# Local attention heads in blocks of 32 queries by 64 keys, two heads transposed together, with the maxima subtracted on VectorE

## The chip, the cores and the metric

The kernel runs on one core of one Trainium2 chip. Five engines work side by side, each through its own list of instructions in order: TensorE (PE in the profile, its weight loads PEld), VectorE (DVE), ScalarE (ACT), GpSimd (POOL) and SyncE (SP), which issues most of the transfers. The metric is the device time of one execution in microseconds (us), lower is better: the median of several runs.

## What is computed

Sparse attention over 8 batches of 576 tokens with 8 heads of 64 elements, then a mixture of 8 experts with the two best per token. Half of the heads are *local*: a query sees itself and the 31 keys before it. The other half are *strided*: a query sees the earlier keys with the same position modulo 32.

```python
# q, k, v: (8, 8, 576, 64) float32; stride = 32; scale = 1 / sqrt(64)
scores = scale * np.matmul(q, k.transpose(0, 1, 3, 2))
rel = pos[:, None] - pos[None, :]
mask_local = (rel >= 0) & (rel < stride)
mask_strided = (rel >= 0) & (pos[None, :] % stride == pos[:, None] % stride)
masks = [mask_local if h < H // 2 else mask_strided for h in range(H)]
scores = np.where(masks, scores, -1e9)
scores = scores - np.max(scores, axis=-1, keepdims=True)
attn = np.exp(scores)
attn = attn / (np.sum(attn, axis=-1, keepdims=True) + 1e-09)
attn_out = np.matmul(attn, v)

# x: attn_out as (4608, 512); noisy top-2 of 8 experts
noisy = x @ w_gate + np.log1p(np.exp(x @ w_noise)) * noise
# out = sum over the two best experts e: weight * (relu(x @ w1[e]) @ w2[e])
```

## The kernel before

**One planned program.** Every step of the kernel is a `Piece` with an engine (or "ANY", which is ACT or DVE), an assumed duration, the tiles that it reads and writes, and a rank. `issue_all` is a list scheduler that runs while the program is built: it takes the piece that can start first by the assumed durations and writes its instructions at the end of that engine's list. So each engine has a fixed order that follows from the planned durations, and on the chip it goes through it in order. A change of one assumed duration can change the order of much else. The eight banks of PSUM are given out piece by piece. When the plan has TensorE wait in the first 170 us, it puts in matmuls of zeros (L401).

**Attention.** A unit is two heads of one batch, local or strided; there are 32 units, four to a batch (two local, two strided), and 16 of them are local. For a unit, `loads` (L435) fetches q, k and v; `prep` (L491) transposes q and k on TensorE so that the head dimension lies on partitions, with the first head on partitions 0 to 63 and the second on 64 to 127. After a batch's four units `route` computes the gate (L785), the two best experts and the place of each token in the experts' lists, and scatters 12 groups of entries from POOL (L875).

For a local unit the program does this:

- The values of the two heads are loaded in one transfer (L493) to partitions 32 to 95, in 18 blocks of 64 tokens (9 for each head); one copy (`front`, L317 on ACT or L320 on DVE, 32 partitions by 17 x 64 elements) puts the last 32 tokens of each block in front of the next, on partitions 0 to 31. A block of 64 queries so has 96 keys.
- `products` (L587 to 618) writes the mask into two banks of PSUM, one for each head, with bfloat16 matmuls (L601: 6 of them, of 96, 384 and 480 columns), and adds the scores (L608: 18 matmuls of 64 queries by 96 keys). These are matmuls on a quarter of the array, 64 rows by 64 columns; the two heads use the two halves of its rows, even and odd blocks the two halves of its columns. TensorE runs a float32 matmul as two instructions, so the trace has 36.
- `item` (L620 to 702) runs for each head. DVE takes the maxima of five groups of 96 scores (L635). ACT makes the exponentials with the maximum as bias, which is one number for each partition, so every group has an instruction of its own (L639, four for each head; L641, two more of 64 partitions, which put the last group of both heads into the second head's tile). TensorE transposes the groups (L649, four for the first head, five for the second), ACT or DVE copies the result out of PSUM (`aT`, L317 or L320), TensorE multiplies by the values and a column of ones (L668, 8 matmuls for each head with 96 rows by 64 columns of the array; L673, 2 more for the last group), and DVE adds 1e-9 to the sums (L678, L680), takes reciprocals (L683, L685) and scales (L689, L697) into `xo`.
- `finish` stores `xo` (L714) and transposes it for the gate (L735, L739).

The strided units go through the same `item`, with 72 keys instead of 96.

**Experts.** Seven jobs of the experts need only the tokens of earlier batches. Their matmuls (first layer L1317, second L1397) are filled in between those of attention from the fourth batch's gate on, and after the last gate the rest follows. Later jobs use a first layer with fewer products (L1221).

## Time and profile before

| | |
|---|---|
| median of 3 runs | 1063.34 us (1061.49 to 1064.67) |
| the profiled execution | 1060.7 us, of which the span of the program is 1058.7 us |
| mean granted TensorE clock | 0.991 of full speed |
| TensorE, VectorE, ScalarE, GpSimd busy | 98%, 69%, 50%, 51% of the span |
| moved by the transfers | 134.43 MB, 127 GB/s over the span |
| gates of the eight batches begin at | 43.1, 73.6, 103.5, 135.1, 175.5, 215.5, 258.2, 302.6 us |
| first matmul of an expert | 136.5 us |

Busy time of an engine is the share of time in which it has an instruction under way. Matmuls are pipelined and their ends in the trace are modelled, so the time that TensorE spends on something is read from the starts: from the first start of a group of matmuls to the start of whatever comes next. In rows of the timeline the columns are the start, the time from first start to last end, the engine, the line, the operation, out<-in, the form and the number of instructions merged in the row. In rows that group instructions the last numbers are the busy time in us, the mean duration of one in ns, and the idle time before them.

### The profile page before, as it was taken

What the parts mean: (1) busy time and instruction counts of PE and PEld (TensorE: products, weight loads), DVE (VectorE), ACT (ScalarE), POOL (GpSimd) and SP (SyncE); (2) the same over time, 40 slices, a digit from 0 to 9 for tenths busy, and PEclk for the clock granted to TensorE, in tenths of its full rate; (3) what the DMA queues carried; (4) which work ended last, traced back from release to release, by engine and by line L of the source; (5) the groups of instructions that cost most, each with busy time, mean ns of one, the idle gap of its engine ahead of it and who ended that gap; (6) DMA issues with size and microseconds to landing.
All of it is one profiled execution on the core that took longest, in us unless ns stands there. A gap on an engine that the chain in (4) does not pass through costs nothing.

```text
span 1058.7 us, 23340 instructions
## 1 busy us (share of the span) xinstructions
PE 1032.9 (98%) x8465; PEld 907.9 (86%) x8465; DVE 726.6 (69%) x1828; ACT 533.3 (50%) x1255; POOL 541.0 (51%) x637
## 2 busy tenths in 40 slices
PE   8899999999999999999898999999999999999997
PEld 6687798988898899888788898989889888989895
DVE  6789985877653124557999487849783977687451
ACT  6888986877643223435555244516342543445220
POOL 1045443623536455756677666766666466641212
PEclk9999999999999999999899999999999999999999
DMA  9969988899665233543655425342724372342312
GB/s 209 223 144 216 270 197 228 220 245 252 175 163 131 52 50 74 142 109 74 162 112 148 65 79 124 106 68 72 167 61 69 83 167 49 76 99 56 39 31 73
DMA packets 165046, 134.43 MB, mean 127 GB/s; under 512 B 48728, under 2 KB 133208, under 8 KB 164904
## 3 DMA queue, kind: packets, MB, share of 16 engines
q1 hardware_dynamic: 142040, 92.30, 33.8%
q0 software_dynamic: 22864, 40.25, 20.1%
q8 instruction: 88, 1.44, 0.6%
q14 instruction: 54, 0.44, 0.1%
HBM read 94.15 MB, written 39.39 MB: 126 GB/s over the span
## 4 chain that ended last, share of the span: by engine, by line
PE 82%; DVE 7%; DMA 4%; ACT 4%; issue 2%; SPq 0%; POOL 0%; POOLq 0%; DVEq 0%; ACTq 0%
PE bankF L1397 6%; PE bankD L1397 5%; PE bankH L1397 5%; PE bankA L1397 5%; PE bankC L1397 4%; PE bankE L1397 4%; PE bankB L1397 4%; PE bankB L1221 3%; PE bankE L1221 3%; PE bankG L1221 3%; PE bankD L1221 3%; PE bankC L1221 3%; PE bankG L1397 3%; PE bankA L1221 3%; PE bankH L1221 3%; PE bankF L1221 2%
## 5 line engine op out<-in xcount | busy, mean ns | idle before, releaser
L1082 POOL DMA_INDIRECT xg<-x_dram,gxx x240 | 257.6, 1073 | 127.9 <-issue 36.1
L1434 POOL DMA_INDIRECT out_dram<-prev,tabt x80 | 131.2, 1640 | 185.1 <-ACT prev L1425 120.1
L875 POOL DMA_INDIRECT tab<-ent,addr x96 | 92.9, 968 | 63.9 <-issue 21.8
L1157 DVE STREAM_TRANSPOSE XR<-xg 128x512 f32<-128x512 f32 (+1 forms) x55 | 56.4, 1043 | 44.1 <-DMA xg<-x_dram,gxx 44.0
L962 DVE TENSOR_TENSOR w2lo<-wraw,w2hi 128x512 fp32r<-128x512 f32 x80 | 52.7, 684 | 34.2 <-ACT w2hi L961 33.4
L1397 PE MATMUL bankF<-w2hi,hp 128*128 128x512 f32 x176 | 57.0, 395 | 0.0
L961 ACT CAST w2hi<-wraw 128x512 fp32r<-128x512 f32 x80 | 46.8, 619 | 17.1 <-DMA wraw<-in_moe_w_dram 3.6
L1281 ACT ACTIVATE hp<-CC 128x864 fp32r<-128x864 f32 (+1 forms) x44 | 40.9, 959 | 27.7 <-DVE CC L1244 27.3
L1253 DVE SCALAR_TENSOR_TENSOR hp<-CC,hp 128x864 fp32r<-128x864 f32 (+1 forms) x44 | 47.0, 1096 | 0.5 <-ACT hp L1281 0.4
L1397 PEld LDWEIGHTS bankF<-w2hi,hp 128*128 128x128 f32 x176 | 33.0, 187 | 8.0
L863 POOL COPY ent<-wt 96x12 f32<-96x12 f32 x8 | 1.6, 206 | 74.5 <-DVE wt L857 68.3
L1163 ACT CAST xThi<-XR 128x1152 fp32r<-128x1152 f32 (+1 forms) x22 | 26.6, 1208 | 21.3 <-DVE XR L1177 21.3
L1397 PE MATMUL bankH<-w2hi,hp 128*128 128x512 f32 x112 | 36.3, 395 | 0.0
L1397 PE MATMUL bankF<-w2lo,hp 128*128 128x512 f32 x88 | 34.8, 395 | 0.0
L1002 ACT CAST fhi<-wraw 128x512 fp32r<-128x512 f32 (+1 forms) x48 | 23.1, 510 | 18.4 <-PE bankH L1221 4.0
L1397 PE MATMUL bankD<-w2hi,hp 128*128 128x512 f32 x96 | 31.2, 395 | 0.0
L1397 PE MATMUL bankC<-w2hi,hp 128*128 128x512 f32 x96 | 31.1, 395 | 0.0
L1165 DVE TENSOR_TENSOR xTlo<-XR,xThi 128x1152 fp32r<-128x1152 f32 (+1 forms) x22 | 30.8, 1416 | 0.0
L1397 PE MATMUL bankA<-w2hi,hp 128*128 128x512 f32 x88 | 29.1, 395 | 0.0
L1397 PE MATMUL bankE<-w2hi,hp 128*128 128x512 f32 x88 | 29.1, 395 | 0.0
L1397 PE MATMUL bankB<-w2hi,hp 128*128 128x512 f32 x88 | 29.1, 395 | 0.0
L1163 ACT CAST xBhi<-XR 128x576 fp32r<-128x576 f32 (+3 forms) x22 | 19.8, 948 | 13.0 <-PE bankA L1221 2.7
(883 smaller groups left out, 3735.0 us busy)
## 6 DMA issues: line engine op xcount, KB each, us to landing
wraw<-in_moe_w_dram SPq DMA_DIRECT2D x160, 256.0 KB
out_dram<-zeros SPq DMA_DIRECT2D x12, 768.0 KB
v_l<-in_v_dram SPq DMA_DIRECT2D x16, 288.0 KB
ks<-in_k_dram SPq DMA_DIRECT2D x13, 320.0 KB
qs<-in_q_dram SPq DMA_DIRECT2D x13, 320.0 KB
x_dram<-xo SPq DMA_DIRECT2D x32, 128.0 KB
x_dram<-xo SPq DMA_DIRECT2D x16, 256.0 KB
raw<-in_k_dram SPq DMA_DIRECT2D x14, 288.0 KB
```

The source lines that it names most:

```text
L875: st = nc.gpsimd.indirect_dma_start(out=tab, out_offset=bass.IndirectOffsetOnAxis(ap=s["addr"].t[:, t, kk:kk + 1], axis=0), in_=s["ent"].t ...
L961: Piece("ACT", act(512) + 30, lambda o: nc.scalar.copy(hi.t, raw.t), rank, read=[raw], alloc=[hi], expert=True)
L962: Piece("DVE", dve(512), lambda o: nc.vector.tensor_tensor(lo.t, raw.t, hi.t.bitcast(F32), ALU.subtract), rank, read=[raw, hi], alloc=[lo] ...
L1082: dma(lambda o, g=g: nc.gpsimd.indirect_dma_start(out=xg.t[:, g, :], out_offset=None, in_=x_dram[:4 * known, :], in_offset=bass.IndirectOf ...
L1157: nc.vector.transpose(dst, xg.t[:, :ng, :].rearrange("p g (i c) -> p g c i", c=ND))
L1163: Piece("ACT", act(n_) + 30, lambda o: nc.scalar.copy(dst(hi.t), src()), rank, read=srcs, expert=True, **{how: [hi]})
L1165: Piece("DVE", dve(n_), lambda o: nc.vector.tensor_tensor(dst(lo.t), src(), dst(hi.t).bitcast(F32), ALU.subtract), rank, read=[*srcs, hi], ...
L1221: nc.tensor.matmul(bank.t[:, :w], x.t[:, m, 128 * kk:128 * kk + 128], moving(y, kk)[:, :w], start=start and q == 0, stop=stop and q == len ...
L1253: nc.vector.scalar_tensor_tensor(dst, src, 0.0, hi.bitcast(F32), op0=ALU.max, op1=ALU.subtract)
L1281: step("ACT", act(3 * w) + 30, lambda o, i=i: nc.scalar.activation(HP[i].t[:, 0, w:4 * w], CC[i].t[:, :3 * w], AF.Relu), read=[CC[i]], wri ...
L1397: nc.tensor.matmul(ps.t, stationary(f, p[0]), W2[n][f][p[1]].t, start=(m == 0), stop=(m == len(todo) - 1))
L1434: st = nc.gpsimd.indirect_dma_start(out=out[:known, :], out_offset=bass.IndirectOffsetOnAxis(ap=tb.t[:rows, i, 0:1], axis=0), in_=pv.t[:ro ...
```

## The change

Local units no longer go through `item`. They have a function of their own, `pair`, for both heads at once, in blocks of 32 queries by 64 keys (`KW` is 64 instead of 96, and there are `NS` = 18 blocks for each head).

- The values lie as blocks of 64 keys, the first head on partitions 0 to 63 and the second on 64 to 127. They are loaded with two transfers of half the size, and the copy that puts the 32 tokens before in front is made once for each head, each as large as the one copy was.
- The mask takes 10 matmuls (64, 256 and 320 columns), the scores 36 matmuls of 32 queries by 64 keys. Each uses an eighth of the array, 64 rows by 32 columns: head by rows, block number modulo 4 by columns.
- DVE takes the maxima of both heads (five groups of 64 each), then subtracts them from the scores with one `tensor_tensor` for each head, which moves 5 x 64 elements from PSUM to SBUF. ACT makes the exponentials of a head with one instruction of 5 x 64 elements in place.
- The two heads' groups lie next to each other in `ex`, so five transposes of 128 x 128 turn both heads. They go out of PSUM in two copies, of 3 and 2 groups.
- The values take 40 matmuls with 64 rows and 32 columns of the array, into one bank for each head. Block 17 and the two unused places of the last group multiply the same values.
- Two instructions add 1e-9, one takes all reciprocals, two scale 5 x 64 elements each.
- The planned durations of these pieces are new: 780 for the mask and scores (1160 before), 650 for the values (656 for a head and 230 more before).

The core of the diff:

```diff
-    KW = QB + STRIDE
+    KW = 2 * STRIDE
+    NS = S // STRIDE
...
-    v_l = [keep.tile([KW, 2, NBL, D + 1], F32, name=f"v_l{i}") for i in range(2)]
+    v_l = [keep.tile([2 * KW, NS, D + 1], F32, name=f"v_l{i}") for i in range(2)]
...
-            put("v", slot, [(lambda t: t[STRIDE:].rearrange("p h n d -> p (h n) d")[:, :, :D], v, base,
-                             [[D, QB], [QB * D, 2 * NBL], [1, D]], 294912)], True)
+            put("v", slot, [(lambda t, h=h: t[KW * h + STRIDE:KW * h + KW, :, :D], v, base + h * S * D,
+                             [[D, STRIDE], [STRIDE * D, NS], [1, D]], 147456) for h in range(2)], True)
...
+            for h in range(2):
+                def front(o, h=h):
+                    copy(o.e, slot.t[KW * h:KW * h + STRIDE, 1:, :D], slot.t[KW * h + STRIDE:KW * h + KW, :NS - 1, :D])
+                Piece("ANY", {"ACT": act(64 * (NS - 1)) + 100, "DVE": 700}, front, rank, read=[slot], write=[slot])
...
+                for g in range(4):
+                    for b, r in enumerate(halves):
+                        for n0, n1, mk in ((0, 1, 0), (1, 5, 1)) if g == 0 else ((0, 5, 1),):
+                            nc.tensor.matmul(sv[b][STRIDE * g:STRIDE * g + STRIDE, n0:n1, :], twin[r, :STRIDE],
+                                             mask_l2[r, mk:mk + 1, :].to_broadcast([QB, n1 - n0, w]),
+                                             start=(n0 == 0), stop=False, skip_group_check=True)
+                for m in range(NS):
+                    g = m % 4
+                    for b, r in enumerate(halves):
+                        nc.tensor.matmul(sv[b][STRIDE * g:STRIDE * g + STRIDE, m // 4, :],
+                                         qT.t.rearrange("r n x -> r (n x)")[r, STRIDE * m:STRIDE * m + STRIDE],
+                                         kT.t[r, STRIDE * m:STRIDE * m + KW], start=False, stop=True, skip_group_check=True)
...
+    def pair(u, scs, L, xo, rank):
...
+        for h in range(2):
+            Piece("DVE", 120 + dve(5 * w), lambda o, h=h: nc.vector.tensor_reduce(mxs[h].t, view(h), AX.X, ALU.max, negate=True),
+                  rank, read=[scs[h]], alloc=[mxs[h]])
+        for h in range(2):
+            Piece("DVE", 140 + 1.05 * 5 * w, lambda o, h=h: nc.vector.tensor_tensor(
+                exv()[:, :, h, :], view(h), mxs[h].t[:, :, None].to_broadcast([128, 5, w]), ALU.add), rank,
+                  read=[scs[h], mxs[h]], loose=bool(h), **{"write" if h else "alloc": [ex]})
+            Piece("ACT", act(5 * w) + 80, lambda o, h=h: nc.scalar.activation(exv()[:, :, h, :], exv()[:, :, h, :], AF.Exp),
+                  rank, read=[ex], write=[ex])
+        for c, m in (0, 3), (3, 2):
...
+                for n in range(m):
+                    nc.tensor.transpose(tp.t[:, 128 * n:128 * n + 128], exv()[:, c + n, :, :].rearrange("r h c -> r (h c)"), ident)
...
+            for n in range(5):
+                for g in range(4):
+                    for h, r in enumerate(halves):
+                        nc.tensor.matmul(of(h)[STRIDE * g:STRIDE * g + STRIDE, n, :], aT.t[r, n, STRIDE * g:STRIDE * g + STRIDE],
+                                         L["v"].t[r, min(4 * n + g, NS - 1), :], start=True, stop=True)
+        Piece("PE", 5 * 118 + 60, values, rank, read=[aT, L["v"]], psum=po)
```

**Where instructions move.** The program is planned anew, so all lists change. Two places show how. The first is VectorE in the second and third batch. Before, the list has one head of a local unit (`rs`, `xo_146`), the next unit's maxima and the route's addresses:

```order
L635 TENSOR_REDUCE mx<-bankE 128x5
L868 TENSOR_TENSOR oh<-oh,ns 96x96
L869 TENSOR_REDUCE addr_f<-oh 96x12
L870 CAST addr<-addr_f 96x12
L678 TENSOR_SCALAR rs<-bankB 128x4
L680 TENSOR_SCALAR rs<-bankB 64x2
L635 TENSOR_REDUCE mx<-bankC 128x5
L683 RECIPROCAL rs<-rs 128x4
L685 RECIPROCAL rs<-rs 64x2
```

Now, in a like place, both maxima (L720) and both subtractions (L723) of a local unit stand there, with the end of a strided unit (L686 to L701) between them:

```order
L720 TENSOR_REDUCE mx<-bankG 128x5
L720 TENSOR_REDUCE mx<-bankD 128x5
L723 TENSOR_TENSOR ex<-bankG,mx 128x5x64
L686 TENSOR_SCALAR rs<-bankE 128x4
L688 TENSOR_SCALAR rs<-bankE 64x2
L723 TENSOR_TENSOR ex<-bankD,mx 128x5x64
L691 RECIPROCAL rs<-rs 128x4
L693 RECIPROCAL rs<-rs 64x2
L322 COPY kT_s<-kT_s 64x4x8
L696 TENSOR_TENSOR xo_144<-bankE,rs 128x2x2x64
L701 TENSOR_TENSOR xo_144<-bankE,rs 64x128
```

VectorE so has one more step between a local unit's scores and its exponentials, and the second head's subtraction stands behind two steps of another unit.

The second place is TensorE ahead of the first expert matmul. Before, both transposes of gathered tokens (L1118, from `xg`) come ahead of the fourth batch's gate, which follows 31 rows behind these and is itself followed at once by the first expert matmul:

```order
L1118 MATMUL bankD<-ident,xg 128x128 x4
L649 MATMUL bankF<-ident,ex 72x128 x4
L739 MATMUL bankA<-ident,xo_144 128x128 x4
L649 MATMUL bankB<-ident,ex 72x128 x4
L1118 MATMUL bankC<-ident,xg 128x128 x4
L735 MATMUL bankE<-ident,xo_144 128x128
L668 MATMUL bankG<-v_s_140,aT 64x65 x8
```

Now the gate (L840) comes ahead of the second of them (L1173), and steps of the fifth batch stand between the gate and the first expert matmul (L1372):

```order
L1173 MATMUL bankF<-ident,xg 128x128 x4
L840 MATMUL bankE<-xT,wg 32x192 x12
L658 MATMUL bankA<-ident,ex 72x128
L562 MATMUL bankG<-ident,qs 128x72 x4
L558 MATMUL bankD<-ident,ord 128x96 x3
L1173 MATMUL bankC<-ident,xg 128x128 x4
L676 MATMUL bankH<-v_s_140,aT 64x65 x8
L680 MATMUL bankH<-v_142,aT 64x65 x2
L847 MATMUL bankB<-ident,lgT 96x96 x2
L733 MATMUL bankF<-ident,ex 128x128 x3
L558 MATMUL bankA<-ident,ord 128x96 x3
L1372 MATMUL bankE<-xhi,w1hi 128x256
```

Attention is thus further along, by a gate and some steps, when the first tokens for an expert are transposed. In both orders nine local and nine strided units have their scores ahead of that gate. Ahead of the last gate stand 288 first-layer matmuls of the experts instead of 324, and 144 of the second layer as before.

More of the change, by code (lines that the diff above doesn't have):

```diff
@@ L180 @@
     for i in range(2):
[L181 to L182 removed]
+        nc.vector.memset(v_l[i][:, :, D:D + 1], 1.0)
+        for h in range(2):
+            nc.vector.memset(v_l[i][KW * h:KW * h + STRIDE, 0, :], 0.0)
         nc.vector.memset(v_0[i][QB:], 0.0)
@@ L513, in loads @@
             slot = R["v_l"].new()
-            put("v", slot, [(lambda t: t[STRIDE:].rearrange("p h n d -> p (h n) d")[:, :, :D], v, base,
-                             [[D, QB], [QB * D, 2 * NBL], [1, D]], 294912)], True)
-            def front(o):
-                vv = slot.t.rearrange("p h n d -> p (h n) d")
-                copy(o.e, vv[:STRIDE, 1:, :D], vv[QB:, :2 * NBL - 1, :D])
-            Piece("ANY", {"ACT": act(64 * (2 * NBL - 1)), "DVE": 640}, front, rank, read=[slot], write=[slot])
+            put("v", slot, [(lambda t, h=h: t[KW * h + STRIDE:KW * h + KW, :, :D], v, base + h * S * D,
[4 more added lines that the diff above has]
+                Piece("ANY", {"ACT": act(64 * (NS - 1)) + 100, "DVE": 700}, front, rank, read=[slot], write=[slot])
         else:
@@ L605, in product @@
                 r = halves[b]
-                rhs = kT.t[r, QB * blk:QB * blk + KW] if local else kT.t[r, blk, :]
-                q0 = 0 if local or blk == NBL - 1 else G0
-                nc.tensor.matmul(sv[b][halves[half], s, :], qT.t[r, blk, q0:q0 + QB], rhs, start=False,
+                q0 = 0 if blk == NBL - 1 else G0
+                nc.tensor.matmul(sv[b][halves[half], s, :], qT.t[r, blk, q0:q0 + QB], kT.t[r, blk, :], start=False,
                                  stop=True, skip_group_check=True)
@@ L615, in scores @@
                 product(b, 4, b, NBL - 1)
-        o = Piece("PE", 20 + 10 * w / 4.8 + 5 * (188 if local else 144), scores, rank, read=[kT, qT], psum=sc)
+        o = Piece("PE", 780 if local else 20 + 10 * w / 4.8 + 5 * 144, scores, rank, read=[kT, qT], psum=sc)
         o.order += in_turn[-1:]
@@ L621, in item @@
     def item(u, i, scs, mxs, L, xo, rank):
-        local = units[u][2]
         nb = 4 + i
-        w = KW if local else G
+        w = G
         sc, mx, ex = scs[i], R["mx"].new(), R["ex"].new()
@@ L665, in values @@
                 for half in range(2):
-                    rhs = L["v"].t[:w, i, 2 * s + half, :] if local else L["v"].t[:w, s // 2, 4 * (s % 2) + 2 * half + i, :]
-                    nc.tensor.matmul(main()[64 * half:64 * half + 64, s, :],
-                                     aT.t[:w, s, 64 * half:64 * half + 64], rhs, start=True, stop=True)
+                    nc.tensor.matmul(main()[64 * half:64 * half + 64, s, :], aT.t[:w, s, 64 * half:64 * half + 64],
+                                     L["v"].t[:w, s // 2, 4 * (s % 2) + 2 * half + i, :], start=True, stop=True)
@@ L670, in values @@
             if nb > 4:
                 for h in range(2):
-                    rhs = L["v"].t[:, h, NBL - 1, :] if local else L["v0"].t[:, h, :]
-                    nc.tensor.matmul(extra()[:, h, :], aT.t[:w, 4, 64 * h:64 * h + 64], rhs, start=True, stop=True)
-        Piece("PE", 4 * 164 + 230 * (nb > 4), values, rank, read=[aT, L["v"]] + ([] if local or nb == 4 else [L["v0"]]),
+                    nc.tensor.matmul(extra()[:, h, :], aT.t[:w, 4, 64 * h:64 * h + 64], L["v0"].t[:, h, :],
+                                     start=True, stop=True)
@@ L1520 @@
         scs, mxs = products(u, *KQ[u], rank), []
-        for i in range(2):
+        if units[u][2]:
+            pair(u, scs, LL[u], xo, rank)
+        for i in range(0 if units[u][2] else 2):
             item(u, i, scs, mxs, LL[u], xo, rank + 5 * i)
```

64 lines of the change are left out of this document (41 added, 23 removed).

## The prediction

> **What bounds the kernel now.** I read the page's chain first, then the stages by windows, then who waits in the stage that the change touches.
>
> ```profile
> PE 82%; DVE 7%; DMA 4%; ACT 4%; issue 2%; SPq 0%; POOL 0%; POOLq 0%; DVEq 0%; ACTq 0%
> ```
>
> The chain that ended last is TensorE's for 82% of the span. The windows say where it is not. Their columns are the length, then PE, PEld, DVE, ACT and POOL busy in us (instructions), the granted clock, the DMA share and GB/s.
>
> ```profile
> 74.00:136.00 62.00, 57.73 (x1027) 47.03 (x1024) 57.10 (x232) 56.50 (x179) 29.25 (x56) 1.00 0.99 237
> 136.00:303.00 167.00, 166.71 (x2188) 146.49 (x2183) 116.53 (x457) 122.13 (x366) 69.55 (x129) 1.00 0.85 214
> 303.00:490.00 187.00, 187.00 (x1078) 169.03 (x1072) 79.39 (x181) 62.69 (x127) 107.00 (x121) 1.00 0.44 97
> 490.00:580.00 90.00, 84.10 (x488) 74.18 (x487) 88.25 (x166) 52.49 (x97) 63.33 (x58) 0.94 0.55 136
> ```
>
> Three things are to be seen. Up to 136 us, the first four batches, there is attention alone: TensorE's 57.73 us hold matmuls of zeros, while VectorE (57.10 of 62) and ScalarE (56.50) are over nine tenths full and the transfers are at 0.99. From 136 to 303 us attention and expert matmuls share TensorE, which is busy for 166.71 of 167 us, VectorE and ScalarE for 70% and 73%. From 303 to 490 us TensorE works without a gap on what is left. So TensorE's total work from the first expert matmul on sets when the rest begins; the stretch from 490 us on, where VectorE is full, comes behind it and shifts with it. TensorE's whole waiting for other engines between 136 and 303 us is one row:
>
> ```profile
> PE bankH L1317 <- ACT qT_l L318: 0.2, 1, 0.2
> ```
>
> The view names no load of attention that an engine waits for in that stage. A microsecond taken from TensorE there is a microsecond off the end, unless a new wait takes it.
>
> **TensorE: scores and mask.** The rows are TensorE's timeline of one local unit in the third batch: start, time to the last end, what.
>
> ```profile
> 77.25 0.23 PE L601 MATMUL bankA<-mask_l,twin 64*64 64x96 bf16 x1
> ...
> 77.48 0.24 PE L608 MATMUL bankA<-kT_l,qT_l 64*64 64x96 f32 x1
> ...
> 77.56 0.24 PE L608 MATMUL bankA<-kT_l,qT_l 64*64 64x96 f32 x1
> ...
> 78.23 0.24 PE L608 MATMUL bankH<-kT_l,qT_l 64*64 64x96 f32 x1
> 78.41 0.66 PE L739 MATMUL bankF<-ident,xo 128*128 128x128 f32 x4
> ```
>
> From 77.25 to 77.48 the masks take 0.23 us, from 77.48 to 78.41 the scores 0.93. Groups of four matmuls, one on each quarter of the array, follow each other every 0.08 us (77.48 to 77.56): the time is that of 96 columns streaming, whatever the neighbours do. Ten such steps make 0.82, the rest, 0.11, is the end of the last. The new matmuls have 64 columns, so 0.08 x 64 / 96 = 0.055 us a step. They fill eight tiles at once if eight run at once: blocks 0 to 15 take 8 steps, 16 and 17 two more, 0.55 + 0.11 = 0.66. A tile's mask shrinks from 480 columns to 320: 0.23 x 320 / 480 = 0.155. Together 0.82 after 1.16.
>
> **TensorE: transposes and values.** Another local unit, both heads:
>
> ```profile
> 230.53 0.69 PE L668 MATMUL bankC<-v_l,aT 96*64 96x65 f32 x16
> 231.15 0.64 PE L649 MATMUL bankB<-ident,ex 128*96 128x128 f32 x4
> 231.63 0.41 PE L556 MATMUL bankE<-ident,ord 96*128 96x96 f32 x3
> ...
> 234.63 0.69 PE L668 MATMUL bankD<-v_l,aT 96*64 96x65 f32 x16
> 235.14 0.40 PE L673 MATMUL bankD<-v_l,aT 96*64 96x65 f32 x4
> 235.47 0.63 PE L649 MATMUL bankC<-ident,ex 128*72 128x128 f32 x4
> ```
>
> Four transposes take 231.63 - 231.15 = 0.48 us, 0.12 each: nine are 1.08, five of them 0.60; the moved columns are 128 either way. The values take 0.62 and 0.51 for the heads and 0.33 for the last group, 1.46. New: 80 instructions, ten steps of eight with 65 columns, 10 x 0.056 + 0.07 for the end = 0.63. The sum for a local unit is 1.16 + 1.08 + 1.46 = 3.70 before and 0.82 + 0.60 + 0.63 = 2.05 after: 1.65 less.
>
> **Do eight tiles run at once?** No row of before has eight. The nearest are strided scores, 72 columns on four tiles:
>
> ```profile
> 84.65 0.19 PE L601 MATMUL bankC<-mask_s,twin 64*64 64x72 bf16 x1
> ...
> 84.70 0.25 PE L608 MATMUL bankD<-kT_s,qT_s 64*64 64x72 f32 x1
> ...
> 84.77 0.22 PE L608 MATMUL bankC<-kT_s,qT_s 64*64 64x72 f32 x1
> ...
> 85.02 0.22 PE L608 MATMUL bankC<-kT_s,qT_s 64*64 64x72 f32 x1
> ```
>
> From 84.77 to 85.02 sixteen matmuls start, one every 15.6 ns, which is the closest that is sustained. But from 84.65 to 84.70 eight start, 7 ns apart, with their weight loads in between, and eight in 55 ns are what the new form needs. The gate shows that 32-column tiles run side by side:
>
> ```profile
> 73.61 1.50 PE L785 MATMUL bankD<-xT,wg 128*32 128x192 f32 x24
> ```
>
> Its 24 matmuls of 192 columns end after 1.50 us; one after another they would take 24 x 192 x 0.08 / 96 = 3.84, so its three column tiles overlap. Three of the four column tiles and both halves of the rows are thus seen, though not eight tiles together. The bounds are 7 ns and 15.6 ns for a matmul; I take 7, since the limit that shows in every row is streaming and not issue.
>
> A rule that speaks against the change: the Trainium skill, "TensorE: Matmul & The Clock Gate", section "Wait — 56ns, not 53.3ns?", says that starts of matmuls never come closer than about 25 ns, however few the columns. By it the 152 score and value matmuls of a unit would take 3.8 us, and the kernel would be slower by some 8 us. This trace does not bear it out: the rows above have 15.6 ns sustained and 7 in bursts.
>
> In both orders seven local units' scores and eight units' values stand behind the fourth gate, so about 7.5 units: 7.5 x 1.65 = 12.4 us off.
>
> **ScalarE and VectorE.** Rows by form, first ScalarE's (60 to 136 us), then VectorE's (60 to 303 us); the last numbers are busy us, mean ns, idle before.
>
> ```profile
> L639 ACT ACTIVATE ex<-bankG,mx 128x96 f32<-128x96 f32 x8 | 2.1, 342 | 0.4 <-DVE mx L635 0.4
> L641 ACT ACTIVATE ex<-bankG,mx 64x96 f32<-64x96 f32 x2 | 0.7, 351 | 0.0
> L317 ACT COPY v_l<-v_l 32x1088 f32<-32x1088 f32 x3 | 3.3, 1099 | 0.1
> L317 ACT COPY xT<-bankF 128x512 f32<-128x512 f32 x3 | 1.7, 581 | 0.3 <-PE bankF L739 0.3
> L317 ACT COPY xT<-bankF 128x64 f32<-128x64 f32 x3 | 0.6, 212 | 0.0
> ```
> ```profile
> L635 DVE TENSOR_REDUCE mx<-bankA 128x5 f32<-128x480 f32 x5 | 3.3, 651 | 0.4 <-issue 0.4
> L689 DVE TENSOR_TENSOR xo<-bankB,rs 128x256 f32<-128x256 f32 x7 | 2.9, 409 | 0.0
> L697 DVE TENSOR_TENSOR xo<-bankB,rs 64x128 f32<-64x128 f32 x9 | 2.5, 274 | 0.0
> L320 DVE COPY v_l<-v_l 32x1088 f32<-32x1088 f32 x3 | 2.2, 744 | 0.1
> L678 DVE TENSOR_SCALAR rs<-bankH 128x4 f32<-128x4 f32 x11 | 1.7, 151 | 0.0
> L320 DVE COPY aT<-bankG 96x512 f32<-96x512 f32 x2 | 1.4, 688 | 0.2
> ```
>
> Ten exponentials, 2.1 + 0.7 = 2.8 us, become two of 320 elements; an element costs (581 - 212) / 448 = 0.82 ns, so two take 2 x (212 + 256 x 0.82) = 0.84: -1.96. VectorE's element costs (409 - 274) / 128 = 1.05 ns. Maxima and scaling were 2 x 0.651 + 2 x 0.409 + 0.274 = 2.39; now the maxima are 2 x 0.483, and subtraction and scaling four times 0.476: 2.87, +0.48. Six small steps (0.15) become three: -0.45. The copies `aT`, on either engine, go from 2 x 0.69 for 512 columns and 0.28 for 128 to 0.55 for 384 and 0.41 for 256, by the same 1.05 ns: -0.70. The second copy in front of the values adds 0.74 on VectorE or 1.10 on ScalarE, 0.95 in the mean. The sum is -1.68 us for a unit, or 0.84 for each of the two engines, which share what either can do.
>
> Between 136 and 303 us that hides behind TensorE. Before 136 us it counts, where both engines are full: from 74 to 136 us, two batches, four local units, 4 x 0.84 = 3.4 us. Ends: nothing, if the transfers at 0.99 hold the stage, and 6.7 if all eight local units count. I take 3.4.
>
> **Edits costed at nothing.** The second load of the values adds an issue of at most the one it is split from to SyncE's list, behind which nothing waits after 136 us. The longer wait for a unit's exponentials (VectorE's subtraction behind two steps of another unit, 0.3 us) is hidden by other units' matmuls while TensorE has expert work; without that cover it would be 16 x 0.3 = 5 us at most. The transfers of 136 to 303 us have to fit in 155: 0.85 x 167 / 155 = 0.92, below the 0.99 shown.
>
> **New waits.** TensorE waits 0.3 of 167 us where ScalarE and VectorE are 71% full, and 4.3 of 62 (6.9%) where they are 92% full. Afterwards they are (116.5 + 122.1 - 8 x 1.68) / (2 x 155) = 73% full: on the line between the two that is 0.6% of 155, so I take 1 us, between 0 and 11.
>
> **The sum.** -12.4 - 3.4 + 1 = -14.8 against the profiled execution's own 1060.7 us: 1045.9. The median of the runs shown is 2.6 above that execution, so 1048.5.
>
> **Rivals.** *Half packed (0.13):* eight tiles do not overlap more than four did, 15.6 ns a matmul. Mask, ends and transposes keep 0.155 + 0.18 + 0.60 = 0.935 us, 152 matmuls take 2.37: a unit takes 3.31, only 0.39 less. 7.5 x 0.39 + 3.4 - 1 = 5.3 off: 1058. Against it stand the starts 7 ns apart.
>
> *The gain turns into waiting (0.12):* the joint chain (two maxima, two subtractions, two exponentials before the first transpose) makes TensorE wait from 136 us on as it did before that, 6.9% of 155 = 10.7: 15.8 - 10.7 = 5.1 off, 1058. For it speaks that 36 fewer expert matmuls stand ahead of the last gate to fill with; against it the 73%.
>
> *Slower (0.09):* small tiles start no closer than their kind does now: 20 ns for scores (four in 0.08), 32 for values (0.51 / 16). Then 72 x 20 + 80 x 32 = 4.0 us, 4.94 for a unit against 3.70, 7.5 x 1.24 = 9.3 more; the early stage, with its zeros, neither gains nor loses: 1072. It decides from 18.2 ns a matmul on: (3.70 - 0.935) / 152.
>
> **Numbers.** The forecast has 0.66: 1048.5. About 0.3% (3.2 us, also the spread of the runs before) is what a measurement can tell. Faster: the forecast and most of the two rivals at 1058, 0.84; within 0.3%: the rest of them, 0.07; slower 0.09. Downwards the range takes all eight units (6.7) and no new wait, 1044, and half the spread of the runs: 1042. Upwards it takes both rivals at 1058 with the same: 1060.
>
> **What would show it.** In the new trace a local unit's scores (L605) should take 0.66 us from first start to the next work, its values (L747) 0.63; starts eight at a time within 55 ns. The first expert matmul should start near 133 us, the last gate near 284 (12.4 and 3.4 earlier, and 36 expert matmuls later in the order), and TensorE should be over 98% busy between. It is wrong if a step of eight takes over 0.1 us, if TensorE's waits there exceed 4 us, or if the stretch to 490 us does not begin earlier by what was saved.

## The result, and the profile after

The changed kernel takes 1071.85 us (median of 12 runs, 1063.6 to 1076.7), the kernel before 1064.2 beside it (1059.9 to 1066.8): a ratio of 1.0072, with an interval from 1.0049 to 1.0096. It is slower by about 0.7%, where 1.4% less was forecast. The profiled execution took 1072.1 us, its span is 1070.4 (1058.7 before), its mean clock 0.988.

The page of the kernel before has these rows for the engines and for the queue that brings TensorE's code:

```profile
PE 1032.9 (98%) x8465; PEld 907.9 (86%) x8465; DVE 726.6 (69%) x1828; ACT 533.3 (50%) x1255; POOL 541.0 (51%) x637
q8 instruction: 88, 1.44, 0.6%
```

and the page of the changed kernel, with its chain:

```profile
PE 1025.4 (96%) x9743; PEld 899.2 (84%) x9743; DVE 719.8 (67%) x1785; ACT 521.7 (49%) x1140; POOL 539.0 (50%) x637
q8 instruction: 98, 1.61, 0.6%
PE 84%; DVE 6%; ACT 4%; DMA 3%; issue 2%; POOL 0%; POOLq 0%; DVEq 0%; ACTq 0%; SPq 0%
```

The chain is TensorE's as before (84% after 82%), but TensorE is busy for 7.5 us less, and yet the span is 11.7 us longer: it waits more. It also has 1278 more matmuls and as many more weight loads, and the code queue moves ten more packets (98 after 88). The windows, cut as in the prediction, say where:

```profile
74.00:136.00 62.00, 51.61 (x1279) 41.47 (x1280) 47.66 (x203) 51.33 (x140) 23.91 (x50) 1.00 0.96 190
136.00:303.00 167.00, 155.86 (x2861) 135.72 (x2860) 121.37 (x456) 117.15 (x315) 72.26 (x138) 0.99 0.87 210
303.00:490.00 187.00, 187.00 (x1055) 167.68 (x1046) 76.71 (x171) 61.84 (x124) 106.09 (x120) 1.00 0.51 117
490.00:580.00 90.00, 84.00 (x497) 73.41 (x496) 81.89 (x158) 49.75 (x93) 63.56 (x55) 0.96 0.54 132
```

TensorE fell from 57.73 to 51.61 and from 166.71 to 155.86 of 167: the stage that had no gap now has 11 us of them. The windows hold earlier work than before, because the changed kernel runs late; up to the first expert matmul, which in both has nine local and nine strided units' scores ahead of it, VectorE is busy for 108.0 us (114.5 before) and ScalarE for 110.3 (112.4), so both did become lighter. The first expert matmul starts at 149.3 us (136.5 before), the last gate at 309.4 (302.6). TensorE's waits up to there, the longest kinds of the changed kernel:

```profile
PE bankB L747 <- issue: 2.6, 1, 2.6
PE bankD L618 <- issue: 2.4, 1, 2.4
PE bankE L605 <- issue: 2.0, 1, 2.0
PE bankH L558 <- ACT ord L319: 2.0, 1, 2.0
PE bankF L1173 <- issue: 2.0, 1, 2.0
PE bankD L562 <- DMA vraw<-in_v_dram: 1.9, 1, 1.9
PE bankE L562 <- DMA ks<-in_k_dram: 1.8, 1, 1.8
PE bankB L605 <- issue: 1.5, 1, 1.5
```

and of the kernel before:

```profile
PE bankH L668 <- issue: 1.8, 1, 1.8
PE bankG L739 <- DVE xo L692: 1.7, 1, 1.7
PE bankH L668 <- DVE aT L320: 1.2, 2, 0.9
```

"Issue" is a wait that nothing in the profile explains. The changed kernel has 12.1 us of it up to the last gate, the kernel before 1.8. One of these waits stands in the middle of a unit's 80 value matmuls, which need nothing more at that point:

```profile
57.34 0.21 PE L747 MATMUL bankB<-v_l,aT 64*32 64x65 f32 x1 [2.59 <-issue]
```

I counted all of TensorE's instructions in the trace from the start of the program to each such wait over 0.3 us: weight loads, matmuls, and those in which it waits for other engines (36 of the first 1985). The wait that ends at 57.34 begins at instruction 1985, the others of the changed kernel at 961, 5569, 6849, 8129 and 9665, the one before at 961. All are 193 modulo 256. And each ends 2.2 to 2.8 us after a packet of the code queue has started (the packet of 54.72 us for the wait that ends at 57.34). Whatever the instruction is, the wait stands at the same place in a block of 256: TensorE has run out of code.

The second finding is the bursts themselves. The scores of one unit in the changed kernel:

```profile
64.80 0.22 PE L605 MATMUL bankG<-kT_l,qT_l 64*32 64x64 f32 x1
...
64.85 0.22 PE L605 MATMUL bankG<-kT_l,qT_l 64*32 64x64 f32 x1
...
64.91 0.22 PE L605 MATMUL bankG<-kT_l,qT_l 64*32 64x64 f32 x1
...
65.33 0.24 PE L605 MATMUL bankG<-kT_l,qT_l 64*32 64x64 f32 x2
...
65.67 0.30 PE L658 MATMUL bankF<-ident,ex 128*72 128x128 f32 x1
```

The first two steps of eight take 0.055 us each (64.80, 64.85, 64.91), just as predicted, so eight tiles do run at once. After some 20 matmuls the pace falls: from the 22nd to the 72nd one starts every 11 ns (the medians of 13 units: number 22 starts 0.174 us and number 72 0.730 us behind the first). Ten mask matmuls stand right ahead of these. The values have none ahead, and there the breaks, of 27 and 57 ns, come after the 32nd and 33rd matmul in 15 of 16 units. So some 32 matmuls, 64 instructions with their weight loads, start close together, and the rest come slowly. The scores take 0.88 us to the next work and the values 0.97, where 0.66 and 0.63 were predicted.

### The profile page after: what moved, and what is told of

Read it like the earlier page. It is cut to its first block, busy times and chain, and to the rows that moved or that the text cites. A ratio compares the mean times of both kernels' runs of the same rounds, so it can differ in the third digit from the quotient of the medians.

```text
span 1070.4 us, 25743 instructions
## 1 busy us (share of the span) xinstructions
PE 1025.4 (96%) x9743; PEld 899.2 (84%) x9743; DVE 719.8 (67%) x1785; ACT 521.7 (49%) x1140; POOL 539.0 (50%) x637
## 4 chain that ended last, share of the span: by engine, by line
PE 84%; DVE 6%; ACT 4%; DMA 3%; issue 2%; POOL 0%; POOLq 0%; DVEq 0%; ACTq 0%; SPq 0%
PE bankD L1452 7%; PE bankE L1452 5%; PE bankA L1452 5%; PE bankG L1452 5%; PE bankF L1452 5%; PE bankB L1452 4%; PE bankH L1452 4%; PE bankF L1276 3%; PE bankB L1276 3%; PE bankE L1276 3%; PE bankC L1276 3%; PE bankG L1276 3%; PE bankC L1452 3%; PE bankA L1276 3%; PE bankH L1276 3%; PE bankD L1276 2%
## 5 line engine op out<-in xcount | busy, mean ns | idle before, releaser
L1137 POOL DMA_INDIRECT xg<-x_dram,gxx x240 | 257.2, 1072 | 128.4 <-issue 36.0
L1452 PE MATMUL bankD<-w2hi,hp 128*128 128x512 f32 x176 | 57.2, 396 | 0.0
L1452 PEld LDWEIGHTS bankD<-w2hi,hp 128*128 128x128 f32 x176 | 33.0, 187 | 8.1
L1452 PE MATMUL bankA<-w2hi,hp 128*128 128x512 f32 x112 | 36.4, 396 | 0.0
L1452 PE MATMUL bankD<-w2lo,hp 128*128 128x512 f32 x88 | 34.6, 394 | 0.0
L1452 PE MATMUL bankH<-w2hi,hp 128*128 128x512 f32 x96 | 31.2, 396 | 0.0
L1452 PE MATMUL bankG<-w2hi,hp 128*128 128x512 f32 x88 | 29.1, 396 | 0.0
L1452 PE MATMUL bankF<-w2hi,hp 128*128 128x512 f32 x88 | 29.1, 395 | 0.0
L1130 POOL DMA_INDIRECT xg<-x_dram,gix x16 | 16.2, 1010 | 21.2 <-PE bankG L1372 5.8
```

What stands on the lines that cost most here:

```text
L1137: dma(lambda o, g=g: nc.gpsimd.indirect_dma_start(out=xg.t[:, g, :], out_offset=None, in_=x_dram[:4 * known, :], in_offset=bass.IndirectOf ...
L1452: nc.tensor.matmul(ps.t, stationary(f, p[0]), W2[n][f][p[1]].t, start=(m == 0), stop=(m == len(todo) - 1))
```

## The experiments

Two theories were tested. *Code* (and *supply*): small matmuls use up TensorE's instructions faster than they come, which slows the bursts and stalls TensorE where a page of 256 instructions ends. These are two effects, the pace inside a burst and the stall at the end of a page. *Loads*: the split load of the values and a new order bring q, k and v late. Rivals of the same kind were the second copy in front of the values, and the planner's order as such. Where an edit is said to hold the order, all planned durations stand as they were, so every engine's list is the same but for the edit. The runs fell on two kinds of chip: on most, the kernel before took 1058 to 1072 us; in six of the runs it took 1095 to 1107, and TensorE there had stalls of 0.4 us, often 0.7 us apart, at any instruction number. Each ratio is to the kernel before on the same chip, but those six are not set beside the others.

**Fewer instructions for the same columns (a_fewer).**

```diff
-for m in range(NS):           # 36 score matmuls of 64 columns
+for g in range(4):            # 8 of 320, on the same eight tiles
...
-matmul(of(h)[.., n, :], aT.t[r, n, ..], L["v"].t[r, min(4 * n + g, NS - 1), :])
+matmul(of(h)[.., :, :], aT.t[r, 0, ..], L["v"].t[r, :5, :])
```

> The changed kernel with the order of every engine held, but each tile of a local unit's scores and values gets its five blocks of columns in one matmul (320 and 325 columns, 8 matmuls instead of 36 and 8 instead of 40); the weights of the first block are used for all five, so the numbers are not those of the reference. The same columns stream through the same eight tiles with a fifth of the instructions. Theory 'code': TensorE's stalls named issue sit at multiples of 256 of its instructions, so it runs dry at a page of code when small matmuls use the instructions up faster than the next page comes; the granted clock then halves. It expects the issue stalls up to the last gate to fall from 12.1 us (9 of them) to under 4, no half clock between 30 and 41 us, scores of a unit 0.6 to 0.7 us and values 0.6 to 0.7 to the next work (0.88 and 0.97 now), first expert matmul at 137 to 143 us (149.3 now), ratio to before 0.988 to 0.998. Theory 'loads': the early stage is late because the split load of the values and the new order bring q, k and v late. It expects the waits for transfers (7.1 us up to 140 us) to stay, the first expert matmul at 146 or later and a ratio of 1.000 to 1.005 from TensorE's shorter time alone.

Measured: 0.985 (0.981 to 0.989), 1048.4 us, a larger gain than theory *code* had forecast. No issue stall over 0.3 us up to the last gate, first expert matmul at 138.2 us, last gate at 285.0. Its timeline:

```profile
68.18 0.43 PE L604 MATMUL bankC<-kT_l,qT_l 64*32 64x320 f32 x1
...
68.45 0.43 PE L604 MATMUL bankC<-kT_l,qT_l 64*32 64x320 f32 x1
...
68.83 0.28 PE L676 MATMUL bankB<-v_s,aT 72*64 72x65 f32 x2
```

```profile
136.00:303.00 167.00, 165.36 (x1953) 139.46 (x1951) 127.34 (x492) 118.68 (x317) 79.95 (x144) 1.00 0.93 226
```

The scores take 0.65 us (68.18 to 68.83) and the values 0.71, and TensorE is busy for 165.36 of 167 us again. TensorE's waits for transfers up to the last gate fell from 5.5 to 2.0 us although the loads are split as in the changed kernel, so the split does not make them late, and theory *loads* is out. That they came late because TensorE, which frees their places, was late is likely, but not shown by itself. The half clock went between 30 and 41 us as theory *code* expected, but 20.5 us of half clock stand elsewhere before the last gate (17.1 in the changed kernel, 3.4 before), behind other waits. So the clock is not what sets the two apart. What stays are the waits for ScalarE: up to the first expert matmul they are 11.6 us, 8.3 in the changed kernel and 3.4 before. The longest in a_fewer:

```profile
PE bankH L558 <- ACT ord L319: 2.3, 1, 2.3
PE bankE L562 <- ACT ex L648: 2.1, 1, 2.1
```

**As many more instructions in the kernel before (b_more).**

```diff
+for j in range(40):   # in the scores, and 40 more in the second head's values
+    nc.tensor.matmul(sc[b].t[32 * g:32 * g + 32, 500:501], twin[..], mask_l2[.., 0, :1], start=True, stop=True)
```

> The kernel before with its order held and 80 more matmuls of one column in each local unit (40 ahead of the masks, 40 ahead of the second head's values), as many instructions as the change adds, with no other work changed. Theory 'code': the issue stalls up to the last gate rise from 1.8 us to 6 us or more, at multiples of 256 instructions, some followed by half clock; with 80 x 7 to 15 ns of TensorE's own time (0.6 to 1.2 us for a unit, eight units in the full stage: 5 to 10 us) the ratio is 1.012 to 1.025. Theory 'loads': TensorE's own time alone, issue stalls as before (1 or 2), ratio 1.004 to 1.010.

Measured: 1.0138 (1.0097 to 1.0179). Its page and its waits up to 310 us:

```profile
PE 1045.8 (97%) x9745; PEld 920.9 (86%) x9745; DVE 728.2 (68%) x1828; ACT 534.3 (50%) x1255; POOL 544.5 (51%) x637
q8 instruction: 98, 1.61, 0.6%
```
```profile
PE bankG L556 <- issue: 3.5, 1, 3.5
...
PE bankF L612 <- issue: 1.2, 1, 1.2
...
PE bankE L612 <- issue: 1.0, 1, 1.0
PE bankD L605 <- issue: 1.0, 1, 1.0
```

Four stalls of 6.7 us in sum, at instructions 4033, 5569, 1729 and 1217, all 193 modulo 256, 4.9 us more than the 1.8 of the kernel before. Most of the rest of the 17.1 us by which the span grew is TensorE's own (12.9 us more busy): forty one-column matmuls take 0.36 us, 9 ns each. With as many instructions as the change has, the kernel before stalls at the same places of a page, though for 6.7 us and not 12.1.

**Is it columns or instructions? (a_narrow)** Order and instructions held; each score matmul streams 16 columns instead of 64:

```diff
-kT.t[r, STRIDE * m:STRIDE * m + KW]
+kT.t[r, STRIDE * m:STRIDE * m + 16]
```

> The changed kernel with its order and its instructions held, but each of the 36 score matmuls has 16 columns instead of 64 (the last 48 keys of a block get no score, so the numbers are not those of the reference). Theory 'supply' (once some 30 matmuls that stand ready are used up, small matmuls come no faster than their instructions do, 11 ns and more each): a unit's scores keep 0.75 to 0.9 us to the next work although a quarter of the columns streams. Theory 'stream' (a step of eight is set by its columns): the scores take 0.25 to 0.45 us.

One run: 1077.8 us. The scores take 0.74 us where nothing interrupts them:

```profile
65.00 0.18 PE L605 MATMUL bankG<-kT_l,qT_l 64*32 64x16 f32 x1
...
65.10 0.18 PE L605 MATMUL bankG<-kT_l,qT_l 64*32 64x16 f32 x1
65.19 0.17 PE L605 MATMUL bankD<-kT_l,qT_l 64*32 64x16 f32 x1
...
65.28 0.20 PE L605 MATMUL bankD<-kT_l,qT_l 64*32 64x16 f32 x2
65.30 0.20 PE L605 MATMUL bankG<-kT_l,qT_l 64*32 64x16 f32 x2
65.31 0.20 PE L605 MATMUL bankD<-kT_l,qT_l 64*32 64x16 f32 x2
65.33 0.20 PE L605 MATMUL bankG<-kT_l,qT_l 64*32 64x16 f32 x2
...
65.74 0.30 PE L658 MATMUL bankF<-ident,ex 128*72 128x128 f32 x1
```

A quarter of the columns saves 0.14 us of 0.88. The first 23 start within 0.10 us (65.00 to 65.10), then comes a break of 0.085 us, and behind it pairs start every 16.7 ns, as they do in stretches of the changed kernel's bursts. So the slow pace is not that of the columns. Every matmul has its own weight load here, as in all runs, and no run takes the loads away alone; against them as the limit speaks that the loads, too, start 3.5 ns apart while the first matmuls do. What sets the slow pace the runs leave open; that it comes with the number of instructions and not of columns they show. There are eight issue stalls over 0.3 us, 15.3 us with the small ones: theory *supply*, a hair below its lower end for the scores.

**Where fewer instructions help, and where not.** First on the chip with the 0.4 us stalls (the kernel before took 1100 us), then again beside a_fewer on one of the others. b_fewer treats the kernel before as a_fewer treats the changed one; a_few_s takes only the scores.

```diff
+matmul(sv[b][halves[half], :, :], qT.t[r, half, :], kT.t[r, :5 * w])              # b_fewer, 4 for 18
+matmul(main()[64 * half:.., :, :], aT.t[:w, 0, ..], L["v"].t[:w, i, :4, :])       # and 6 for 18
```

> The kernel before with its order held and the same treatment as the fewer-instructions kernel of the change: each quarter-array tile of a local unit gets its blocks in one matmul (480 columns of scores, 260 of values; 4 matmuls instead of 18 and 6 instead of 18), with the first block's weights for all, so the numbers are not those of the reference. Theory 'supply': matmuls of 96 columns on four tiles take 20 ns each, which their instructions keep up with, so little changes: scores 0.9 us and values 1.3 to 1.5 as before, ratio 0.995 to 1.002. Rival 'all alike' (fewer instructions help any kernel of this kind, and the change's tiles are not what made them scarce): ratio under 0.992.

> The changed kernel with its order held, only the scores in 8 matmuls of 320 columns (with the first blocks' weights, so the numbers are not those of the reference), the values in 40 as changed. A unit so has 56 records of TensorE fewer than now and 8 fewer than the kernel before. Theory 'code': both bursts use up pages, so taking one away takes away half or more of the stalls: issue stalls up to the last gate 2 to 6 us against 12.1, scores 0.66 us, ratio 0.990 to 0.999. Rival 'pace' (the slow bursts themselves cost, the stalls happen anyway): issue stalls over 8 us, ratio 1.001 to 1.006.

Measured there: b_fewer 0.9888 (0.986 to 0.992), which was the rival's number, and a_few_s 0.9892 (0.985 to 0.993). Since most of their issue waits were of the kind that the other traces don't have, I ran them again:

> The kernel before with its order held and its local scores and values in fewer, wider matmuls, as in the run b_fewer, whose chip was disturbed (the kernel before took 1100 us there, with stalls of 0.4 us that no other trace has). Theory 'supply': the matmuls of before keep up with their instructions, ratio 0.995 to 1.002. Rival 'all alike': as on the other chip, under 0.992, so that scarce instructions were no property of the change.

> The changed kernel with its order held and the scores alone in 8 matmuls, again because of the disturbed chip. Theory 'code': issue stalls up to the last gate 2 to 6 us, all at 193 of 256 instructions, ratio 0.992 to 1.000. Rival 'pace': stalls over 8 us, ratio 1.001 to 1.006.

> The changed kernel with scores and values in 8 matmuls each once more, beside b_fewer on the same chip. Theory 'supply': 0.985 within its interval (0.981 to 0.989), 1% or more under b_fewer: with instructions enough, the change gains what its columns say. Rival 'all alike': within 0.5% of b_fewer.

Measured: b_fewer 0.9982 (0.9965 to 1.0000), without an issue stall; a_few_s 1.001 (0.999 to 1.003) with five, 6.4 us in sum; a_fewer 0.9867 (0.9825 to 0.991) with one of 1.8 us. On these chips fewer instructions give the kernel before 0.2% and the changed kernel 2%. What the two have left between them, 1.2% (0.9867 / 0.9982), is what the change is worth in these two orders when instructions are plenty. a_few_s is between its two forecasts: about half the small matmuls away, half the stalls away. (A unit has 111 matmuls there, 24 more than in the kernel before and not 8 fewer, as its first expectation says.) Its waits up to 310 us begin with

```profile
PE bankB L747 <- issue: 2.6, 1, 2.6
PE bankH L558 <- ACT ord L319: 2.3, 1, 2.3
PE bankH L747 <- issue: 1.5, 1, 1.5
```

both stalls in the values, the dense burst that was left.

**The second copy (a_nocopy).** Order held; `front` moves one block for the second head:

```diff
-slot.t[KW * h:KW * h + STRIDE, 1:, :D]
+slot.t[KW * h:KW * h + STRIDE, 1:2 if h else NS, :D]
```

> The changed kernel with its order held, but the second head's copy in front of the values moves one block of 17 (the rest of that head's earlier keys are zeros, so the numbers are not those of the reference). Takes 0.7 us from VectorE or 1.0 us from ScalarE in each local unit. Theory 'copy' (the second copy is what the early stage pays): first expert matmul 3 to 5 us earlier than 149.3, ratio to before 1.002 to 1.004. Theory 'code': under 2 us, ratio 1.005 to 1.009, issue stalls as many as now.

Measured: 1.0113 (1.008 to 1.015), seven issue stalls, first expert matmul at 150.7 us. The copy costs the end nothing; theory *copy* is out. The ratio is above theory *code*'s forecast as well, which the runs do not explain.

**One part alone (b_exp).** In the kernel before, VectorE subtracts and one ScalarE instruction for a head makes the exponentials:

```diff
+nc.vector.tensor_tensor(exv()[:, :4, :], view(sc)[:, :4, :], mx.t[:, :4, None].to_broadcast(..), ALU.add)
+nc.scalar.activation(exv(), exv(), AF.Exp)
```

> The kernel before with one part of the change alone: VectorE subtracts the maxima (384 columns for each head and twice 64 x 96 for the last group) and one ScalarE instruction for each head makes its exponentials; tiles, transposes and values stay. ScalarE loses 1.7 us for a unit (six instructions fewer and more: 2.8 us to 1.1), VectorE gains 1.6. TensorE's instructions stay as they were. Theory 'code': issue stalls as in the kernel before (one or two up to the last gate), ratio 0.997 to 1.004, since what one engine loses the other gains. Rival 'chain' (the subtraction in the chain is what makes TensorE wait): waits for exponentials up to the first expert matmul over 4 us against 1.2, ratio over 1.005.

Measured: 1.0024 (0.9997 to 1.005), no issue stall, but the first expert matmul at 147.5 us and 10.7 us of waits for ScalarE's results up to there (3.4 before), 4.7 of them for exponentials (1.2 before). By time it is theory *code*'s 'no change', by waits the rival's longer chain. Since the order is a new one too, I can't part the two.

**How much is the order? (a_costs, a_costs_again, a_replan, b_replan)** Only planned durations are changed, not one instruction:

```diff
-o = Piece("PE", 780 if local          # 1030 in a_costs, 790 in a_replan
-Piece("PE", 5 * 118 + 60, values      # 970 in a_costs
...
-5 * (188 if local else 144)           # kernel before: 1160 in all
+5 * (190 if local else 144)           # b_replan: 1170
```

> The changed kernel with the planned durations set to what the trace shows: mask and scores 1030 instead of 780, values 970 instead of 650; only the order can change. Theory 'plan' (the order was made for durations that are too short, so loads and chains are mistimed): waits for transfers and for exponentials shrink, first expert matmul before 145 us, ratio 0.995 to 1.003. Theory 'code': the instructions are as many and as dense, so the issue stalls stay above 8 us up to the last gate and the ratio between 1.004 and 1.010.

> The changed kernel with one planned duration changed by 10 ns (mask and scores of a local unit 790 instead of 780); every instruction stays, only the order can change. Theory 'order' (what the changed kernel loses depends on the order that the planner happens to draw): a ratio to before that differs from 1.0072 by 0.003 or more to either side. Theory 'durations' (the corrected durations of the run before helped because they are right): within 0.002 of 1.0072.

> The kernel before with one planned duration changed by 10 ns (mask and scores of a local unit 1170 instead of 1160); every instruction stays, only the order can change. Theory 'order': the order that stood was a good draw, and another costs 0.3 to 1%: ratio 1.003 to 1.010. Rival: an order drawn anew costs nothing, ratio 0.998 to 1.002, so that what the changed kernel lost was not its order.

> The changed kernel with the planned durations 1030 and 970 again: 0.9998 (0.998 to 1.002) in its first run. Theory 'order': the order is the same, so the ratio is the same within 0.003; a ratio over 1.004 would mean that the chip or the moment, not the order, made it 0.7% faster than the change.

Measured: a_costs 0.9998 (0.998 to 1.002), again 1.0017 (0.999 to 1.0045); a_replan 1.0122 (1.007 to 1.017); b_replan 1.0051 (1.0025 to 1.0076). Ten nanoseconds in one planned number moved the kernel before by 0.5%, and the changed kernel by as much, though there the intervals (1.0049 to 1.0096 and 1.007 to 1.017) still overlap. That is nearly what the change itself did. a_costs came out as theory *plan* had forecast by its ratio, its first expert matmul (142.0 us) and its waits for transfers (0.7 us up to the last gate), and theory *code* missed the ratio; but its waits for ScalarE did not shrink. b_replan has no issue stall, but one long wait up to 310 us that the order brings:

```profile
PE bankE L608 <- DVE qT_l L321: 3.2, 1, 3.2
...
PE bankH L369 <- DVE zeros L100: 1.1, 1, 1.1
```

So the measured 0.7% is one draw. Drawn three times, the change gave 1.0072, 1.0122 and 1.0007 (the mean of a_costs' two runs); the kernel before, drawn twice, 1.000 and 1.005. Beside the second of these the best order of the changed kernel would be ahead by 0.4%: by their orders alone the runs show it neither slower nor faster as such. a_costs has four and eight issue stalls in its two profiles (7.1 and 13.2 us), so it isn't the stalls that the better order took away.

**Versions that might beat both (a_costs2, a_split).** a_costs2 plans 1400 and 1350; a_split plans a unit's scores and values as two pieces each, so that other work comes between the halves of the scores.

> The changed kernel with planned durations that also take in the stalls: mask and scores 1400, values 1350 (1030 and 970 gave 0.9998, 780 and 650 gave 1.0072, 790 and 650 gave 1.0122). Theory 'durations': still at or under 1.000, waits for transfers under 1 us. Theory 'order': another draw, anywhere from 0.998 to 1.012; over 1.003 speaks for it. A ratio whose interval lies below 1 would be a version that beats both.

> The changed kernel with the same instructions, but a unit's scores planned as two pieces (masks and nine matmuls, 590; nine matmuls, 440) and its values as two (580 and 390), so that the planner can put other units' work between the halves; it does so in the scores. Theory 'code': a burst that is broken by longer matmuls gives the next page time to come: issue stalls up to the last gate under 6 us against 12.1, the longest first to go, scores' two halves together 0.75 us or less where other work stands between; ratio 0.992 to 1.000, which would beat both. Theory 'order': another draw like the others, stalls 7 to 15 us, ratio 1.000 to 1.012.

> The kernel a_split again, since its first run fell on the disturbed chip (1.0043 there, the kernel before at 1103 us). There only one stall, of 2.1 us, lay at a page boundary. Theory 'density': without the disturbance, stalls at page boundaries up to the last gate are under 6 us and the ratio 0.990 to 0.999, a version that beats both. Theory 'order': a ratio of 1.000 to 1.008.

> The changed kernel itself on the same chip as a_split2: 1.0072 (1.0049 to 1.0096) in its own measurement, with 12.1 us of issue stalls in six places. Theory 'code': the same places again, at 193 of 256 instructions, 8 to 16 us, ratio 1.004 to 1.010; theory 'order' says the same of the ratio.

All four fell on the other kind of chip (the kernel before: 1100 to 1103 us): a_costs2 1.0137 (1.009 to 1.018), a_split 1.0043 (1.001 to 1.007) and 1.0109 (1.006 to 1.0155), the changed kernel itself 1.0003 (0.997 to 1.003). All but one of the changed kernel's stalls were elsewhere than at its six places there:

```profile
PE bankD L605 <- issue: 3.1, 6, 1.4
...
PE bankE L605 <- issue: 2.4, 4, 1.3
...
PE bankA L605 <- issue: 1.7, 4, 0.5
```

Neither version beats the kernel before. Longer planned durations are not better as such: a_costs2, planned longest, is 1.0137 and the changed kernel 1.0003 on chips of the same kind. The expectation for after_again was wrong on both counts. Whether a_split takes away the stalls at page ends stays open: it had only one or two of those, but on a chip where the changed kernel had only one as well.

## Why the prediction was wrong, point by point

**The step that failed** is "I take 7, since the limit that shows in every row is streaming and not issue". The 7 ns were those of instructions that stood ready. Only some 32 matmuls of a burst, the masks included, start that close; the rest of the scores start every 11 ns (0.730 - 0.174 us for 50), and with a quarter of the columns hardly closer. And at the ends of pages of code TensorE stops altogether, for 12.1 us up to the last gate, a cost that the sum has at nothing. A unit's TensorE time is 0.15 + 0.88 + 0.54 + 0.97 = 2.5 us for mask, scores, transposes and values where nothing interrupts it, against 2.05 predicted and 3.70 before; a mean over all units, half clock included, fell by 0.90 us, not 1.65. The transposes (0.60 predicted, 0.54) and the mask (0.155, 0.15) were right, and so were the steps of eight as long as instructions stood ready: a_fewer's scores take 0.66 and its values 0.71.

**TensorE from 136 us on, -12.4:** between the first expert matmul and the last gate TensorE spent 85.7 us on other work than the experts before and 78.8 after: -6.9. The bound at 15.6 ns, with its 0.39 us for a unit, was too far the other way.

**New waits, +1 (0 to 11):** 0.3 us became 7.3, +7.0. It is inside its ends, but by another cause than the one named: 5.4 are issue. Waits for VectorE and ScalarE, whose share gave me the 1, grew by 1.4.

**Early stage, -3.4 (-6.7 to 0):** +12.8, far outside, and the largest miss of the three. VectorE and ScalarE did become lighter, and that was worth nothing: TensorE's waits up to the first expert matmul rose from 11.7 to 24.2 us. Of those, issue went from 1.8 to 6.7, transfers from nothing to 5.2 and ScalarE's results from 3.4 to 8.3. In the same order with far fewer instructions the first expert matmul starts at 138.2 and 134.8 us (a_fewer twice), 11 to 14 us earlier than 149.3, so in this order all of the 12.8 hangs on the instructions. The first of these runs gains 6.4 us of issue, 4.9 of transfers and 3.2 of TensorE's own time, and loses 3.3 to ScalarE. But the 3.4 us do not come either (+1.7 and -1.7), because the waits for ScalarE's results are 11.6 and 10.6 us: lighter engines did not mean shorter chains. Half clock does not decide the stage, since a_fewer has more of it, but some comes with the stalls: the one that ends at 30.70 is followed by 10.2 us, which a window of the changed kernel shows as 0.54:

```profile
30.00:40.00 10.00, 9.15 (x114) 7.34 (x117) 4.65 (x16) 4.82 (x16) 0.00 (x0) 0.54 0.90 200
```

Together -6.9 + 7.0 + 12.8 = 12.9. The expert matmuls ahead of the last gate, 36 fewer, take 6.4 us less, but the stretch from the last gate to the end is only 4.9 longer (761.0 after 756.1), which gives 1.5 back: 11.4 of the 11.7 by which the span grew.

**Edits costed at nothing:** the second load was fairly judged (a_fewer has it, with few waits for transfers). The longer chain of exponentials was not quite: up to the first expert matmul TensorE waits for exponentials for 3.7 us in the changed kernel, 6.1 and 4.1 in a_fewer and 4.7 in b_exp, after 1.2 before. The growth is within the 5 us that I gave as the most, but it is not nothing; how much of it is the chain and how much the order is open. What I costed at nothing without saying so were the instructions: 1278 matmuls and their weight loads more, 164 instructions in a burst of scores and masks, and an order drawn anew.

**The rivals.** 'Half packed' came nearest in effect, since the sustained 11 ns lie between its 15.6 and my 7, but not in its mechanism: eight tiles do overlap. 'Gain turns into waiting' had roughly the right size of waits for a wrong reason; each alone gave 1058. 'Slower' had the right time, 1072, by luck: its tiles start 20 and 32 ns apart, which they don't. The Trainium skill's rule of 25 ns between starts ("TensorE: Matmul & The Clock Gate", section "Wait — 56ns, not 53.3ns?") is not borne out either: 11 ns are sustained here. Of the three signs of being wrong, the long waits and the late stretch came; a step of eight over 0.1 us did not, as eight at 11 ns take 0.09.

**What can be said of the change.** With instructions plenty and its order held its time is the forecast one, 1048.4 and 1047.3 us against 1048.5. The terms on TensorE hold there: other work than the experts' between the first expert matmul and the last gate falls by 13.0 and 12.7 us (12.4 forecast), and the waits there grow by 1.3 and 3.2 (1). The early stage does not (138 and 135 us, not 133), so that the sum agrees this well is partly luck. As it stands the change is no gain over the kernel before in any of three orders.

## What to carry to other kernels

Cost TensorE's instructions as well as its columns: a burst of matmuls ran at the pace of its columns only for the some 64 instructions that stood ready, and a change that halves the tiles doubles what has to be fetched. Count all of an engine's instructions to the places where it waits for "issue"; here equal remainders modulo 256 gave the wait for code away. Where a planner sets the order, draw the order of the kernel before anew as well before 0.5% is put down to an edit.

## What the runs showed of the hardware

- On the chips without the 0.4 us stalls, every one of the issue stalls over 0.3 us up to 330 us, 52 in ten of the 14 profiles (four have none), begins at a TensorE instruction whose number, all its instructions counted, is 193 modulo 256, and ends 2.2 to 3.6 us after a code packet of 16,384 bytes has started. 1278 more matmuls with their weight loads are 2556 instructions, ten times 256, and the code queue moved ten more packets. The Trainium skill, "Runtime: NRT & Kernel Launch", section "Instruction fetch mechanics", says that code comes in blocks of 16 KiB, 256 instructions, and that this is mostly hidden because instructions are issued more slowly than blocks arrive. The block size agrees; that it is hidden does not hold here, with up to 15.3 us of stalls.
- Eight tiles of 64 rows by 32 columns run at once: 16 matmuls of 320 columns on eight tiles take 0.65 us to the next work.
- Small matmuls with a weight load each start 3.5 to 7 ns apart at first, some 32 of them (64 instructions), and then every 8 to 12 ns in the mean, whether they have 1, 16 or 64 columns (b_more, a_narrow, the changed kernel).
- On some chips the same kernels took 3 to 4% longer, with stalls of 0.4 us in bursts of small matmuls that are not at page ends. What they are, and whether they belong to the chip or to the moment, the runs do not show.
